# Hash attention with a gated feed-forward: where VectorE's decoding of the float64 weights stands in the order

## The chip, the cores and the metric

One core of one Trainium2 chip. The metric is the device time of one execution in microseconds; before the change it is 758.06, the median of three runs (755.7 to 759.31). TensorE (PE) multiplies and transposes, VectorE (DVE), ScalarE (ACT) and GpSimd (POOL) do the elementwise work, SyncE (SP) issues most DMAs. Line numbers L are those of the kernel before, unless the text says that they are of the changed one.

## The reference, cut to what matters

```python
B, H, S, D = 4, 8, 768, 64            # q, k, v: float32
q_bucket = sum((q @ proj > 0) * 2**arange(6));  k_bucket likewise
scores = where(q_bucket == k_bucket.T, q @ k.T / 8, -1e9)
attn = softmax(scores)                # + 1e-9 in the denominator
x = (attn @ v), heads side by side    # (4, 768, 512)
h = relu(x @ w_in)                    # d_ff = 1024
conv = 3-tap convolution of h along the sequence, one tap triple per channel
out = (h * sigmoid(conv)) @ w_out
```

w_in (512 x 1024), the taps and w_out (1024 x 512) arrive as float64. [...]

## The kernel before

**Attention.** The 32 heads are worked in 16 pairs, batch by batch (four pairs make a batch of the input). A pair is 12 *units*: six tiles of 128 queries for each of the two heads, in an order that takes two tiles of one head, two of the other. The main loop runs over units i; in step i it issues, in this order,
- the scores of unit i (`products`, L253: two passes of two matmuls; the second pass carries the low parts and the hash bits, so that a pair of different buckets gets a very low score),
- its row maximum on VectorE, which also moves the scores to SBUF (L266), and the scaled negative of it (L270),
- the transposes of unit i - 3 (L296) and their eviction `at` on ScalarE (L303),
- the exponential of unit i on ScalarE (L273),
- every fourth step, (i - 3) % 4 == 0, a *batch* of products with the values of the four units before (`values`, L322), 24 matmuls; for the first six pairs two transposes that spread the reciprocals of the sums go ahead of them (L317), and x = values times reciprocals follows (L331 on VectorE from the factors rs that ScalarE copied, L327; L332 and L333 on GpSimd make its high and low parts xh and xl). Later pairs are "late": they are normalised before the transposes (L281) and need no spread.

Scores, transposes and hash products share a ring of three PSUM buffers ("S"): the next user of a buffer waits until VectorE or ScalarE has read the last one.

**The next pair's operands.** R holds q and k of one pair, transposed; there is one buffer of it. `prepare` splits R into a high part hi and a low part that overwrites R (L171, L176, GpSimd; DMAs on SP put the parts into Q1, K1, Q2, K2), and multiplies R with the hash projections (`hash`, L186 on TensorE; L189 on VectorE turns the signs to bits, L191 on GpSimd scales them, eight DMAs place them). It goes forward one of seven steps per unit, from unit PREP of a pair on: unit 3 in the first, 2 in the second, 1 in the others. Six units after its start the pair's v and the pair after next's R are asked for; the load of R waits for the last DMA out of the buffer.

**Decoding.** Sixteen blocks of raw weights (128 x 512 float64, 512 KB each) and the taps. For a block, `decode` issues: its size, the absolute value of the high words, on ScalarE (L87); on VectorE five steps: L89 zeroes too small numbers, L91 shifts, L93 joins sign and exponent bits to the shifted mantissa (that is the upper part `up`), L95 keeps the power of two, L97 makes the lower part from the low words. `split_weight` then casts `up` to the high part on ScalarE (L105) and makes the low part in two GpSimd instructions (L107, L109). `background` is called once per unit after the values and lets the blocks under way go on until a step that waits for another engine; a new block begins every 4.1 units (RATE) from unit 6 (W0) on. So the five steps of VectorE stand one or two at a time behind the maxima of several units. The raw loads are issued on SP in units 2, 6, 10, ....

**The feed-forward** of a batch (`ffn`) follows two pairs after its last pair: 16 groups of 12 matmuls (`hidden`, L360), three behind them 9 matmuls each of `output` (L390), with the elementwise work of gate and split between. It runs four times. Blocks that aren't decoded by the first go on in it.

Of the kernel before, what the change touches and what calls it, by code (L numbers as in the profile page):

```python
# [7 lines left out]
F32 = mybir.dt.float32  # L8
# [20 lines left out]
F64_MIN = 2.0 ** -15 * 1.125  # L29
# [5 lines left out]
PREP = (3, 2, 1)  # L35
PREP_N = 6
W0 = 6
RATE = 4.1
HRATE = 2.5
# [4 lines left out]
def lsh_attention_conv_ffn(ctx, tc, qk, v, hw, w_in, conv_w, w_out, consts, ident_in, out):  # L44
# [29 lines left out]
    def decode(raw, n, name):  # L74

        pr = raw.rearrange("p (n two) -> p n two", two=2)
        lo, hi = pr[:, :, 0].bitcast(U32), pr[:, :, 1].bitcast(F32)
        up, low = (ring(wp, bufs, [P, WC], I32, f"w{x}", f"w{x}{name}")[:, :n]
                   for x, bufs in (("u", 3), ("l", 3)))
        upf, lowf = up.bitcast(F32), low.bitcast(F32)
        V = nc.vector
        nc.scalar.activation(lowf, hi, AF.Abs)  # L87
        yield 2
        V.scalar_tensor_tensor(upf, lowf, F64_MIN, hi, ALU.is_ge, ALU.mult)  # L89
        yield 1  # L90
        V.tensor_scalar(low, up, 3, 0x3FFFFFFF, ALU.logical_shift_left, ALU.bitwise_and)  # L91
        yield 0
        V.scalar_tensor_tensor(up, up, -0x40000000, low, ALU.bitwise_and, ALU.bitwise_or)  # L93
        yield 2
        V.tensor_scalar(low, up, -0x800000, None, ALU.bitwise_and)  # L95
        yield 0
        V.scalar_tensor_tensor(lowf, lo, 2.0 ** -52, lowf, ALU.mult, ALU.mult)  # L97
        return upf, lowf

    def split_weight(raw, name):  # L100

        up, low = yield from decode(raw, WC, name)
        yield 2
        blk = weights[name] = cp.tile([P, 2, WC], F32R, tag=f"w{name}", name=f"w{name}")
        nc.scalar.copy(blk[:, 0, :], up)  # L105
        yield 2
        nc.gpsimd.tensor_tensor(up, up, blk[:, 0, :].bitcast(F32), ALU.subtract)  # L107
        yield 1
        nc.gpsimd.tensor_tensor(blk[:, 1, :], up, low, ALU.add)  # L109

    def decode_taps(raw):
        up, low = yield from decode(raw, NFC * 3, "cw")
        nc.vector.tensor_tensor(cw.rearrange("p f k -> p (f k)"), up, low, ALU.add)
# [5 lines left out]
    fetched, splits, step = [], [], [0]  # L119

    def fetch(n):

        for src, name in blocks[:n]:
            raw = cp.tile([P, 2 * WC], I32, tag=f"w{name}", name=f"raw{name}")
            nc.sync.dma_start(raw, src)
            fetched.append((raw, name))
        del blocks[:n]

    def background(rate, stop):

        step[0] += 1
        if rate and fetched and step[0] // rate > (step[0] - 1) // rate:
            splits.append(split_weight(*fetched.pop(0)))
        now = splits[:]
        while now:
            for g in now[:]:
                ended = next(g, None)
                if ended is None:
                    splits.remove(g)
                if ended is None or ended >= stop:  # L140
                    now.remove(g)


    class Pair:
# [61 lines left out]
        def prepare_now(self):  # L206
# [10 lines left out]
            for h in range(2):  # L217
# [9 lines left out]
                bits = ring(wp, 3, [P, WC], I32, "wl", f"bits{nm}_{h}").bitcast(F32)[:, :HS]  # L227
# [78 lines left out]
    def values(pr, qb, ats, rec):  # L306
# [22 lines left out]
        def out():  # L329
            x = ring(wp, 2, [P, QB], F32, "x32", f"x{pr.nm}_{qb}")  # L330
# [14 lines left out]
        rs = ring(wp, 2, [P, QB], F32, "rs", f"rs{pr.nm}_{qb}")  # L345
# [35 lines left out]
    def output(b, half, f, g, acc):  # L381
# [10 lines left out]
        if f == NFC - 1:  # L392
            for m in range(HS // P):
                osb = ring(wp, 3, [P, WC], I32, "wu", f"osb{b}_{half}_{m}").bitcast(F32)
# [9 lines left out]
    def ffn(b, xs, fill, last):  # L404
# [4 lines left out]
        for i in range(len(todo) + FLAG):  # L409
# [8 lines left out]
            background(HRATE, 2)  # L418
# [27 lines left out]
    for i in range(n + LAG):  # L446
# [5 lines left out]
        for high, low in lows:  # L452
            high()
# [108 lines left out]
```

## Time and profile before

| what | value |
|---|---|
| runs | 755.7, 759.31, 758.06 us; median 758.06 |
| the profiled execution's own time | 758.92 us |
| its span, first to last instruction | 757.1 us |
| granted TensorE clock, mean | 0.99 |
| busy: PE, DVE, ACT, POOL | 717.0, 498.0, 511.9, 358.1 us |
| chain that ended last, by engine | PE 77%, DVE 15%, ACT 2%, DMA 2%, POOL 2% |
| first feed-forward begins | at 210.2 us |

A row of the timeline has the start, the length, the engine, the line, the operation, what it writes and reads, and in brackets the engine's idle time before it and what ended that. A row of the waits has who waited for whom, the total, how often, and the longest. In the table of busy times by stretch, each engine's busy us and count follow the stretch's length; the clock, the busy share of the DMA engines and GB/s end the row. The matmuls' ends are modelled.

### The profile page before, as it was taken

To read this page: it belongs to the slowest core of one execution; us is meant where nothing else is said; L and a number is where in the kernel's file an instruction comes from. 1 tells how busy PE (TensorE), PEld (TensorE's weight loads), DVE (VectorE), ACT (ScalarE), POOL (GpSimd) and SP (SyncE) were. 2 spreads that over 40 slices of the span, in tenths; PEclk is the share of its full clock that TensorE was granted. 3 is DMA by queue.
4 is the path that set the end of the run, shared out by engine and by line. 5 is a ranking of instruction groups with operands and counts; after the bars stand their busy time and mean duration, and the time that the engine had idled before them with its cause. 6 is when DMAs were issued, how large, how long until landed. Compare 5 with 4: busy or idle time off the path is not lost.

```text
span 757.1 us, 13345 instructions
## 1 busy us (share of the span) xinstructions
PE 717.0 (95%) x4588; PEld 586.6 (77%) x4588; DVE 498.0 (66%) x1212; ACT 511.9 (68%) x954; POOL 358.1 (47%) x355
## 2 busy tenths in 40 slices
PE   5989989888889999999999999999999999999997
PEld 3867767666679887777779988777779998778986
DVE  7778979778757646566657665666656665554653
ACT  5867777776755558778775547778775556875554
POOL 4345856565555324655735323556653433441222
PEclk8999999999999999999999999999999999999999
DMA  4656486482622103365541302256461211000011
GB/s 139 158 175 199 112 203 172 121 232 67 158 50 63 63 1 105 75 166 153 126 119 34 95 1 104 50 149 154 111 159 40 63 43 62 3 1 1 0 43 42
DMA packets 30355, 72.16 MB, mean 95 GB/s; under 512 B 5936, under 2 KB 7504, under 8 KB 30288
## 3 DMA queue, kind: packets, MB, share of 16 engines
q1 hardware_dynamic: 30000, 71.27, 34.8%
q8 instruction: 36, 0.59, 0.3%
q14 instruction: 31, 0.25, 0.1%
q10 hardware_dynamic: 288, 0.05, 0.0%
HBM read 27.40 MB, written 6.29 MB: 45 GB/s over the span
## 4 chain that ended last, share of the span: by engine, by line
PE 77%; DVE 15%; ACT 2%; DMA 2%; POOL 2%; issue 1%; DVEq 0%; SPq 0%; POOLq 0%; ACTq 0%
PE o L390 18%; PE h L360 17%; PE v L322 15%; PE s L253 13%; PE t L296 13%; DVE e L266 6%; DMA R<-in_qk 2%; PE hash L186 1%; DVE wuo L93 1%; DVE wlo L97 1%; DVE wui L93 1%; DVE st L270 1%; ACT e L273 1%; DVE wli L97 1%; DVE x L331 1%
## 5 line engine op out<-in xcount | busy, mean ns | idle before, releaser
L266 DVE TENSOR_SCALAR_CACHE_REDUCE e<-s 128x768 f32<-128x768 f32 x192 | 183.0, 953 | 87.3 <-PE s L253 80.8
L273 ACT ACTIVATE e<-e,st 128x768 f32<-128x768 f32 x192 | 180.7, 941 | 28.5 <-DVE st L270 13.9
L303 ACT COPY at<-t 128x768 f32<-128x768 f32 x192 | 152.0, 792 | 62.7 <-PE t L296 62.7
L296 PE MATMUL t<-ident,e 128*128 128x128 f32 x1152 | 162.6, 278 | 16.6 <-DVE e L266 14.0
L281 POOL TENSOR_SCALAR e<-e,st 128x768 f32<-128x768 f32 x120 | 109.2, 910 | 126.1 <-ACT at L303 65.0
L296 PEld LDWEIGHTS t<-ident,e 128*128 128x128 f32 x1152 | 130.9, 142 | 43.4 <-DVE e L266 23.7
L369 DVE SCALAR_TENSOR_TENSOR ht<-ht,cw 128x384 f32<-128x384 f32 (+1 forms) x128 | 113.1, 883 | 72.5 <-ACT ht L367 70.3
L379 POOL TENSOR_TENSOR g<-ht,g 128x384 fp32r<-128x384 f32 x64 | 72.9, 1138 | 169.3 <-ACT g L378 137.3
L390 PE MATMUL o<-wo,g 128*128 128x512 f32 x576 | 143.0, 394 | 1.0 <-POOL g L379 1.0
L360 PE MATMUL h<-xh,wi 128*128 128x386 f32 x512 | 142.2, 341 | 1.3 <-ACT ht L365 1.3
L322 PE MATMUL v<-at,v 128*64 128x256 f32 x1152 | 138.1, 385 | 0.0
L390 PEld LDWEIGHTS o<-wo,g 128*128 128x128 f32 x576 | 107.2, 188 | 22.0 <-POOL g L379 1.4
L253 PE MATMUL s<-K,Q 128*128 128x384 f32 x384 | 116.2, 384 | 3.9 <-DVE e L266 2.7
L322 PEld LDWEIGHTS v<-at,v 128*64 128x64 f32 x1152 | 83.2, 138 | 41.6 <-issue 9.2
L253 PE MATMUL s<-k,q 96*128 96x384 f32 x384 | 99.6, 340 | 2.5 <-DVE e L266 2.2
L360 PEld LDWEIGHTS h<-xh,wi 128*128 128x128 f32 x512 | 94.1, 188 | 5.3 <-ACT ht L365 1.8
L372 ACT ACTIVATE ht<-ht 128x384 f32<-128x384 f32 x64 | 33.6, 526 | 90.2 <-DVE ht L369 90.2
L360 PE MATMUL h<-xl,wi 128*128 128x386 f32 x256 | 86.8, 339 | 0.0
L253 PEld LDWEIGHTS s<-K,Q 128*128 128x128 f32 x384 | 58.5, 191 | 33.5 <-issue 18.6
L253 PEld LDWEIGHTS s<-k,q 96*128 96x128 f32 x384 | 70.6, 191 | 3.6 <-ACT q L233 3.1
L373 DVE TENSOR_TENSOR ht<-ht 128x384 f32<-128x384 f32 x64 | 43.1, 674 | 33.9 <-ACT ht L372 33.9
L176 POOL TENSOR_TENSOR R<-R,hi 128x768 fp32r<-128x768 f32 x30 | 59.2, 1973 | 0.2
(75 smaller groups left out, 613.5 us busy)
## 6 DMA issues: line engine op xcount, KB each, us to landing
R<-in_qk SPq DMA_DIRECT2D x15, 768.0 KB
K<-hi SPq DMA_DIRECT2D x60, 192.0 KB
v<-in_v SPq DMA_DIRECT2D x16, 384.0 KB
out<-osb SPq DMA_DIRECT2D x24, 256.0 KB
Q<-hi SPq DMA_DIRECT2D x30, 192.0 KB
q<-hi SPq DMA_DIRECT2D x30, 192.0 KB
Q<-R SPq DMA_DIRECT2D x30, 192.0 KB
k<-R SPq DMA_DIRECT2D x30, 192.0 KB
```

Of the source, the lines that this page charges most:

```text
L176: nc.gpsimd.tensor_tensor(lo, R, hi.bitcast(F32), ALU.subtract)
L253: nc.tensor.matmul(self.sp[:, half, :HS], A[:, h, qs], C[:, h, half * HS:(half + 1) * HS], start=(kk == 0), stop=(kk == 1))
L266: nc.vector.tensor_scalar(self.e.rearrange("p (a b) -> p a b", a=2), self.sp[:, :, :HS], MASKED, None, ALU.max, ALU.max, accum_out=self.st ...
L273: nc.scalar.activation(self.e, self.e, AF.Exp, bias=self.st[:, 1:2], scale=SCALE, accum_out=self.sum)
L281: nc.gpsimd.tensor_scalar(self.e, self.e, self.st[:, 3:4], 0.0, ALU.mult, ALU.add)
L296: nc.tensor.transpose(self.tp[:, c // 3, c % 3 * P:(c % 3 + 1) * P], self.e[:, c * P:(c + 1) * P], ident)
L303: nc.scalar.copy(pr.at[self.h][:, :, :, self.tq * P:(self.tq + 1) * P], self.tp[:, :, :3 * P].rearrange("p j (c q) -> p j c q", c=3))
L322: nc.tensor.matmul(av[h * D:(h + 1) * D, :QB], vt[:, c, h, :], ats[h][:, c // 3, c % 3, :], start=(c == 0), stop=(c == NCK - 1), tile_posi ...
L360: nc.tensor.matmul(hp[:, :HW], w, x[:, c0:c0 + HW], start=(n == 0), stop=(n == 3 * NCC - 1))
L369: nc.vector.scalar_tensor_tensor(t[:, a:z], ht[:, o + k - 1 + a:o + k - 1 + z], cw[:, f, k:k + 1], t[:, a:z], ALU.mult, ALU.add)
L379: nc.gpsimd.tensor_tensor(g[:, 1, :], t, g[:, 0, :].bitcast(F32), ALU.subtract)
L390: nc.tensor.matmul(op, l, r, start=(f == 0 and n == 0), stop=(f == NFC - 1 and n == 2))
```

## The change

- **Decoding in four steps and at one place.** L89 goes. The size is clamped on GpSimd instead (`clamp`), the shift works on the clamped size, and the join takes sign and exponent from the raw high words. The four steps of VectorE are issued only in the units of a batch, 3.75 in the mean (so four, every fourth time three), behind x and the hash bits and ahead of the next unit's maximum, from unit 7 on. Sizes run two blocks ahead, clamps one or two; a block's two GpSimd instructions (`ends`) are issued behind the next block's join.
- **x** (or the low part of a late pair) moves from the unit ahead of the batch into the batch's unit. Its ring and that of the factors have one buffer.
- **The hash** stands ahead of the values in the batch's unit: `prepare` starts at unit 1 in every pair, the hash is in its third step, together with the first low half; R and v are asked for at unit 7. Where a feed-forward comes at a pair's unit 2, the hash falls into it.
- **Raw loads** are issued by ScalarE, in units 1, 3, 5, 7 and then with each batch.
- The rings of `up` and of the sizes have 2 and 5 buffers instead of 3 and 3; the output staging moves from the one to the other.

```diff
-PREP = (3, 2, 1)
+PREP = 1
-W0 = 6
-RATE = 4.1
-HRATE = 2.5
+W0 = 7
+RATE = 3.75
...
-        V.scalar_tensor_tensor(upf, lowf, F64_MIN, hi, ALU.is_ge, ALU.mult)
...
+        def clamp(self):
+            nc.gpsimd.tensor_scalar(self.lowf, self.lowf, F32_MAX, F64_MIN, ALU.min, ALU.max)
+        def upper(self):
+            V, up, low = nc.vector, self.up, self.low
+            V.tensor_scalar(low, low, 3, 0x3FFFFFFF, ALU.logical_shift_left, ALU.bitwise_and)
+            yield
+            V.scalar_tensor_tensor(up, self.hi, -0x40000000, low, ALU.bitwise_and, ALU.bitwise_or)
+            yield
+        def lower(self):
+            V, up, low = nc.vector, self.up, self.low
+            V.tensor_scalar(low, up, -0x800000, None, ALU.bitwise_and)
+            yield
+            V.scalar_tensor_tensor(self.lowf, self.lo, 2.0 ** -52, self.lowf, ALU.mult, ALU.mult)
+            yield
+    def split_weights():
...
+        while todo:
+            d = todo.pop(0)
+            ahead()
+            yield from d.upper()
+            if ends:
+                ends()
+            if len(todo) == 2:
+                todo[-1].clamp()
+            yield from d.lower()
+            blk = weights[d.name] = cp.tile([P, 2, WC], F32R, tag=f"w{d.name}", name=f"w{d.name}")
+            nc.scalar.copy(blk[:, 0, :], d.upf)
+
+            def ends(d=d, blk=blk):
+                nc.gpsimd.tensor_tensor(d.upf, d.upf, blk[:, 0, :].bitcast(F32), ALU.subtract)
+                nc.gpsimd.tensor_tensor(blk[:, 1, :], d.upf, d.lowf, ALU.add)
...
-            nc.sync.dma_start(raw, src)
+            nc.scalar.dma_start(raw, src)
...
-            for now in ((sa, hs), (hs,), (sa,), (), (sb,), (), (sb,)):
+            for now in ((sa,), (), (hs, sa), (hs,), (sb,), (), (sb,)):
...
-            x = ring(wp, 2, [P, QB], F32, "x32", f"x{pr.nm}_{qb}")
+            x = ring(wp, 1, [P, QB], F32, "x32", f"x{pr.nm}_{qb}")
...
-            background(HRATE, 2)
+            background(1)
...
-        for high, low in done:
-            low()
+        if burst:
+            for high, low in lows:
+                low()
+            lows = []
+        if u and k == PREP and pi + 1 < len(pairs):
+            prep[0] = pairs[pi + 1].prepare()
+        next(prep[0], None)
...
+        if burst and i >= W0:
+            background(RATE)
...
-        if i >= W0 - 4:
-            fetch(i % 4 == 2)
-        if i >= 1:
-            background(RATE if i >= W0 else 0, 1)
+        fetch(i % 2 if i < 8 else burst)
```

VectorE's order before, around the first units of the third pair (names: e_2_1_1 is pair 2, query tile 1, head 1; bits_3 the hash bits of pair 3; wu, wl a block's upper and lower parts; the batch of the values is in the unit of e_2_1_1):

```order
L331 TENSOR_TENSOR x_1_1_866<-v_1_1_783,rs_1_1_784 128x256
L189 TENSOR_SCALAR bits_3_881<-hash_3_876,cst 128x384
L266 TENSOR_SCALAR e_2_0_1_894,st_2_0_1_893<-s_2_0_1_888 128x768
L270 TENSOR_SCALAR st_2_0_1_893<-st_2_0_1_893 128x1
L89 SCALAR_TENSOR_TENSOR wui_1_885<-wli_1_886,rawi_1_654 128x512
L266 TENSOR_SCALAR e_2_1_1_927,st_2_1_1_926<-s_2_1_1_921 128x768
L270 TENSOR_SCALAR st_2_1_1_926<-st_2_1_1_926 128x1
L91 TENSOR_SCALAR wli_1_886<-wui_1_885 128x512
L93 SCALAR_TENSOR_TENSOR wui_1_885<-wui_1_885,wli_1_886 128x512
L266 TENSOR_SCALAR e_2_2_0_969,st_2_2_0_967<-s_2_2_0_962 128x768
```

The same place on VectorE in the changed kernel, by its own lines (L299 is the maximum, L364 x, L222 the bits, L95, L97, L102 and L104 the four steps):

```order
L299 TENSOR_SCALAR e_2_1_1_910,st_2_1_1_909<-s_2_1_1_904 128x768
L303 TENSOR_SCALAR st_2_1_1_909<-st_2_1_1_909 128x1
L364 TENSOR_TENSOR x_1_1_924<-v_1_1_788,rs_1_1_789 128x256
L222 TENSOR_SCALAR bits_3_933<-hash_3_928,cst 128x384
L95 TENSOR_SCALAR wli_1_583<-wli_1_583 128x512
L97 SCALAR_TENSOR_TENSOR wui_1_582<-rawi_1_456,wli_1_583 128x512
L102 TENSOR_SCALAR wli_1_583<-wui_1_582 128x512
L104 SCALAR_TENSOR_TENSOR wli_1_583<-rawi_1_456,wli_1_583 128x512
L299 TENSOR_SCALAR e_2_2_0_974,st_2_2_0_972<-s_2_2_0_967 128x768
```

x, the bits and all four steps of a block stand between two maxima, where before one or two steps stood behind each. GpSimd's order in that same unit of the changed kernel (L365 and L366 are xh and xl, L209 the low half, L139 and L140 a block's ends, L90 a clamp, L224 the bits):

```order
L365 TENSOR_SCALAR xh_1_663<-x_1_1_924 128x256
L366 TENSOR_TENSOR xl_1_664<-x_1_1_924,xh_1_663 128x256
L209 TENSOR_TENSOR R_3_722<-R_3_722,hi_3_0_878 128x768
L139 TENSOR_TENSOR wui_0_452<-wui_0_452,wi_0_952 128x512
L140 TENSOR_TENSOR wi_0_952<-wui_0_452,wli_0_453 128x512
L90 TENSOR_SCALAR wli_1_955<-wli_1_955 128x512
L224 TENSOR_SCALAR bits_3_933<-bits_3_933,cst 128x384
```

Everything that GpSimd has to do for x, the next pair and a block follows on x in one run.

TensorE there before (hash_3 is pair 3's hash, t a unit's transposes, v_1_2 the batch):

```order
L186 MATMUL hash_3_876<-R_3_724,hw_sb 32x384 x4
L253 MATMUL s_2_0_1_888<-K_2_375,Q_2_374 128x384 x2
L253 MATMUL s_2_0_1_888<-k_0_75,q_0_73 128x384 x2
L296 MATMUL t_1_5_1_897<-ident,e_1_5_1_791 128x128 x6
L253 MATMUL s_2_1_1_921<-K_2_375,Q_2_374 128x384 x2
L253 MATMUL s_2_1_1_921<-k_0_75,q_0_73 128x384 x2
L296 MATMUL t_2_0_0_930<-ident,e_2_0_0_830 128x128 x6
L317 MATMUL v_1_2_919<-ident,rec_1_5_1_855 128x128 x2
```

And in the changed kernel:

```order
L286 MATMUL s_2_0_1_884<-K_2_340,Q_2_339 128x384 x2
L286 MATMUL s_2_0_1_884<-k_0_75,q_0_73 128x384 x2
L329 MATMUL t_1_5_1_893<-ident,e_1_5_1_796 128x128 x6
L286 MATMUL s_2_1_1_904<-K_2_340,Q_2_339 128x384 x2
L286 MATMUL s_2_1_1_904<-k_0_75,q_0_73 128x384 x2
L329 MATMUL t_2_0_0_913<-ident,e_2_0_0_844 128x128 x6
L219 MATMUL hash_3_928<-R_3_722,hw_sb 32x384 x4
L350 MATMUL v_1_2_902<-ident,rec_1_5_1_867 128x128 x2
```

The hash has moved behind two units' scores, directly ahead of the batch.

More of the change, by code (lines that the diff above doesn't have):

```diff
@@ L72, in lsh_attention_conv_ffn @@
     nc.vector.memset(zero[64:96], 0.0)
[L74 to L109, printed above, removed]
-    def decode_taps(raw):
-        up, low = yield from decode(raw, NFC * 3, "cw")
-        nc.vector.tensor_tensor(cw.rearrange("p f k -> p (f k)"), up, low, ALU.add)
+    class Decode:
+        def __init__(self, raw, n, name):
+            pr, self.name = raw.rearrange("p (n two) -> p n two", two=2), name
+            self.lo, self.hi = pr[:, :, 0].bitcast(U32), pr[:, :, 1]
+            self.up, self.low = (ring(wp, bufs, [P, WC], I32, f"w{x}", f"w{x}{name}")[:, :n]
+                                for x, bufs in (("u", 2), ("l", 5)))
+            self.upf, self.lowf = self.up.bitcast(F32), self.low.bitcast(F32)
+        def size(self):
+            nc.scalar.activation(self.lowf, self.hi.bitcast(F32), AF.Abs)
+        def clamp(self):
[12 more added lines that the diff above has]
+            yield
@@ new lines, in split_weights, with ahead @@
+    def split_weights():
+        todo, ends = [], None
+        def ahead():
+            if fetched:
+                raw, name = fetched.pop(0)
+                todo.append(Decode(raw, WC, name))
+                todo[-1].size()
+        ahead()
+        ahead()
+        yield
+        for d in todo:
+            d.clamp()
+        yield
+        while todo:
+            d = todo.pop(0)
+            ahead()
+            yield from d.upper()
[9 more added lines that the diff above has]
+                nc.gpsimd.tensor_tensor(blk[:, 1, :], d.upf, d.lowf, ALU.add)
+        ends()
@@ L116, in lsh_attention_conv_ffn @@
+    def decode_taps(raw):
+        d = Decode(raw, NFC * 3, "cw")
+        d.size()
+        yield
+        d.clamp()
+        yield
+        yield from d.upper()
+        yield from d.lower()
+        nc.vector.tensor_tensor(cw.rearrange("p f k -> p (f k)"), d.upf, d.lowf, ALU.add)
     blocks = [(w_in[c * P:(c + 1) * P, 2 * n * WC:2 * (n + 1) * WC], f"i{c}_{n}")
@@ L124, in fetch, with background @@
             raw = cp.tile([P, 2 * WC], I32, tag=f"w{name}", name=f"raw{name}")
-            nc.sync.dma_start(raw, src)
+            nc.scalar.dma_start(raw, src)
             fetched.append((raw, name))
         del blocks[:n]
[L129 to L141, printed above, removed]
+    def background(n):
+        due[0] += n
+        while due[0] >= 1:
+            due[0] -= 1
+            next(weights_todo, None)
     class Pair:
@@ L450, in lsh_attention_conv_ffn @@
         pi, k = divmod(i, 2 * NCK)
-        done, outs, lows = lows, [], outs
-        for high, low in lows:
+        burst = AVS[(i - LAG) % 4] > 0
+        for high, low in outs:
             high()
+        lows, outs = lows + outs, []
         wi = (i - LAG) // (2 * NCK)
@@ L458, in lsh_attention_conv_ffn @@
         if ending:
-            for high, low in done + lows:
+            for high, low in lows:
                 low()
-            done, lows = [], []
+            lows = []
         if u:
```

25 lines of the change are left out of this document (14 added, 11 removed).

## The prediction

> **What bounds the kernel now.** I read the page's engine line, then two stretches (the table of busy times by stretch), then the chain and the waits of the first 205 us.
>
> ```profile
> PE 717.0 (95%) x4588; PEld 586.6 (77%) x4588; DVE 498.0 (66%) x1212; ACT 511.9 (68%) x954; POOL 358.1 (47%) x355
> 140.00:160.00 20.00, 16.73 (x125) 13.10 (x124) 15.65 (x34) 14.33 (x27) 15.43 (x15) 1.00 0.54 131
> 300.00:320.00 20.00, 20.00 (x155) 14.92 (x154) 12.20 (x48) 15.90 (x31) 12.29 (x14) 1.00 0.25 58
> ```
>
> TensorE is busy 20.00 of 20 us in the late stretch, where all weights are decoded: nothing that VectorE gives up there can be gained. In the early stretch it is busy 16.73, with VectorE at 15.65 and GpSimd at 15.43. The change can pay only before the first feed-forward stage. There the waits are:
>
> ```profile
> PEld t L296 <- DVE e L266: 23.7, 29, 1.8
> PE t L296 <- DVE e L266: 14.0, 17, 1.4
> DVE wuo L89 <- ACT wlo L87: 9.3, 8, 1.4
> ```
>
> TensorE's next transposes need the PSUM buffer that a unit's maximum (L266) has read, and the maximum stands behind decoding. I measure this stage in periods: from one batch of products with the values to the next, four units later. Each batch begins with two spread transposes (L317).
>
> ```profile
> 24.29 0.38 PE L317 MATMUL v<-ident,rec 128*128 128x128 f32 x2
> 33.19 0.38 PE L317 MATMUL v<-ident,rec 128*128 128x128 f32 x2
> 47.45 0.63 PE L317 MATMUL v<-ident,rec 128*128 128x128 f32 x2
> 212.42 0.38 PE L317 MATMUL v<-ident,rec 128*128 128x128 f32 x2
> L317 PE MATMUL v<-ident,rec x36: 271/273/421, 24.3 to 212.5; 128*128 128x128 f32 x36
> ```
>
> 36 transposes are 18 batches, so 17 periods in 212.42 - 24.29 = 188.1 us, 11.07 each. The first, 33.19 - 24.29 = 8.90, has almost no decoding and no wait: that is TensorE's own price for four units and a batch. The second, 14.26, holds the worst stall:
>
> ```profile
> 39.93 0.38 SPq L158 DMA_DIRECT2D R<-in_qk  x1
> 44.21 0.85 PE L186 MATMUL hash<-R,hw_sb 128*32 128x384 f32 x8 [2.79 <-DMA R<-in_qk]
> ```
>
> If nothing but TensorE counted, the 17 periods would be 17 x 8.90, five hashes of 0.85 (the sixth goes into the feed-forward) and one hidden group in the last period:
>
> ```profile
> 388.75 2.11 PE h L360 x12
> ```
>
> 151.3 + 4.3 + 2.1 = 157.7. At most 30.4 us can be had.
>
> **What sets a period after the change.** VectorE's order in a batch's unit becomes: maximum, x, (hash bits), up to four decode steps, next maximum. TensorE covers this for a while: the batch, the next scores, one set of transposes and another scores. Then it needs the next maximum. So I work out when the decode steps end, first from their prices alone:
>
> ```profile
> 35.63 0.69 DVE L93 SCALAR_TENSOR_TENSOR wui<-wui,wli 128x512 int32<-128x512 int32 x1
> 38.46 0.42 DVE L95 TENSOR_SCALAR wli<-wui 128x512 int32<-128x512 int32 x1
> 38.92 0.69 DVE L97 SCALAR_TENSOR_TENSOR wli<-rawi,wli 128x512 f32<-128x512 uint32 x1
> ```
>
> A block now has two shifts or masks (0.42) and two three-operand steps (0.69): 2.22 us. The removed L89 had the shape of L97. But those rows ran with GpSimd idle. With GpSimd at work:
>
> ```profile
> 45.05 1.28 POOL L107 TENSOR_TENSOR wui<-wui,wi 128x512 f32<-128x512 f32 x1
> 45.21 0.62 DVE L189 TENSOR_SCALAR bits<-hash,cst 128x384 fp32r<-128x384 f32 x1 [2.88 <-DMA rawi<-in_w_in]
> 45.74 1.14 DVE L89 SCALAR_TENSOR_TENSOR wui<-wli,rawi 128x512 f32<-128x512 f32 x1
> 46.32 1.02 POOL L191 TENSOR_SCALAR bits<-bits,cst 128x384 fp32r<-128x384 f32 x1
> 46.80 0.94 DVE L266 TENSOR_SCALAR_CACHE_REDUCE e<-s 128x768 f32<-128x768 f32 x1
> 47.30 1.27 POOL L109 TENSOR_TENSOR wi<-wui,wli 128x512 fp32r<-128x512 f32 x1
> 47.86 0.99 DVE L91 TENSOR_SCALAR wli<-wui 128x512 int32<-128x512 int32 x1
> 48.53 2.01 POOL L176 TENSOR_TENSOR R<-R,hi 128x768 fp32r<-128x768 f32 x1
> 48.89 2.20 DVE L93 SCALAR_TENSOR_TENSOR wui<-wui,wli 128x512 int32<-128x512 int32 x1
> ```
>
> L93 takes 2.20 instead of 0.69: it ends 0.55 behind L176 (51.09 against 50.54). L91 ends 0.28 behind L109 (48.85 against 48.57). GpSimd's next instruction is stretched in turn: L191 ends 0.46 behind L89. The two engines take turns, instruction by instruction. The maximum and the bits, which read PSUM, run at their price all through. So a decode step that meets GpSimd costs the rest of GpSimd's instruction plus 0.28 or 0.55, and after it GpSimd's next instruction goes first.
>
> The Trainium skill (SBUF — State Buffer, section "Who interferes with whom") speaks against bunching the steps: VectorE and GpSimd share one port pair under an exclusive lock, the loser "fully blocks", and a VectorE instruction with at most one SBUF input outside the two-port modes stays free. By uncontended prices alone the sum would reach the 30.4 us above; by that rule whole GpSimd instructions come between the steps, and the sum is the smaller one below. The trace agrees (2.20 beside 0.69, and 0.94 for the maximum).
>
> The other prices, and how GpSimd is filled at that moment:
>
> ```profile
> 55.30 0.17 DVE L287 TENSOR_SCALAR sums<-sums 128x4 f32<-128x4 f32 x1
> 55.60 0.41 DVE L331 TENSOR_TENSOR x<-v,rs 128x256 f32<-128x256 f32 x1
> 56.24 0.41 POOL L332 TENSOR_SCALAR xh<-x 128x256 fp32r<-128x256 f32 x1
> 56.73 0.73 POOL L333 TENSOR_TENSOR xl<-x,xh 128x256 fp32r<-128x256 f32 x1
> L176 POOL TENSOR_TENSOR R<-R,hi x30: 1822/1844/2332, 22.9 to 595.6; 128x768 fp32r<-128x768 f32 x30
> ```
>
> From the start of the maximum: it and its scale 1.06 (46.80 to 47.86), x 0.41, so 1.47. GpSimd's queue behind x is xh (0.41), xl (0.73), then in two batches of three a low half (1.83), then the end of the block before (1.28 and 1.27) and a clamp.
> - *Hash batch* (low half, bits first): bits wait for TensorE's transposes and hash, so the steps begin at 2.25; xl ends at 2.7. Then 0.28 = 3.0, low half 4.8, 0.55 = 5.35, first end 6.65, 0.28 = 6.9, second end 8.2, 0.55 = 8.75.
> - *Batch with a low half, no hash*: one step free 1.9, xh 2.3, 0.55 = 2.85, xl 3.6, 0.28 = 3.85, low half 5.7, 0.55 = 6.25.
> - *Plain batch*: the same with the first end in place of the low half, 5.7.
>
> From there three maxima (3 x 1.06) and the sums (0.30 from 55.30 to 55.60) must still be done before the next batch's maximum: 3.48. Periods: 12.25, 9.75 and 9.2; TensorE's floor is 8.90 (9.75 with a hash).
>
> **The sum.** At 3.75 steps a batch every fourth batch has three: without a hash it falls to the floor, with one it ends at 6.9, period 10.4. Seventeen periods: the first two at the floor (one decode step; then no block's end yet) 17.8; four full hash batches 49.0; one with three steps 10.4; four with a low half 39.0; two at the floor 17.8; three plain 27.6; the last, three steps and the hidden group, 11.0. Total 172.6, against 188.1: **-15.5**.
>
> *Hash and loads.* Pair 2's R is loaded two units earlier and its hash comes one unit later, behind transposes and ahead of the values: the 2.79 and the slow restart behind it (the spread took 0.63, not 0.38) go; both are inside the 14.26. Late next is the low half on GpSimd, which waits for the hash; that is in the hash batch.
>
> *Raw weights on ScalarE's queue.* Four loads fall into the first eight units, two before, and no longer queue behind R:
>
> ```profile
> 1.18 0.45 ACTq L65 DMA_DIRECT2D cst<-in_consts  x1
> 12.71 0.39 SPq L158 DMA_DIRECT2D R<-in_qk  x1
> 13.15 0.47 SPq L125 DMA_DIRECT2D rawi<-in_w_in  x1
> 17.43 0.80 PE L186 MATMUL hash<-R,hw_sb 128*32 128x384 f32 x4 [0.41 <-DMA R<-in_qk]
> ```
>
> The hash waits for R at 17.43. The first raw load is now issued about 14.6 (behind an exponential); if it takes half the engines from then on, R lands up to 17.4 - 14.6 = 2.8 later; if it keeps behind R, 0. I take 1.0, near the lower end since most of R has moved by then: **+1.0**. The Trainium skill (DMA: Bandwidth & Descriptors, "Queues, rings and completion order") says that each DMA engine goes round-robin over the queue rows; by it the term would lie nearer 2.8 and the sum 1.8 smaller. No run here shows two such queues at once. Each issue also holds ScalarE about 0.45 us, 16 times; it falls into the batch, where ScalarE waits for the values anyway; bare, 7.2 us, but only a period already bound by ScalarE would feel it. SP loses 16 issues that delayed R and hi: nothing.
>
> *Sizes, casts, clamps, rings.* The size moves two blocks ahead, so the 9.3 us that L89 waited for ScalarE's L87 are not on the path. The cast still waits for VectorE's upper half; queued behind it on ScalarE are a size, the DMA issue, the factors rs and the next eviction.
>
> ```profile
> 41.70 0.60 ACT L105 CAST wi<-wui 128x512 fp32r<-128x512 f32 x1
> 42.21 0.66 ACT L87 ACTIVATE wli<-rawi 128x512 f32<-128x512 f32 x1
> ```
>
> In the hash batch the upper half is there at 5.35, so these end at 7.1 (0.60 + 0.66 + 0.45); the eviction's buffer is wanted by scores after 9: nothing. On GpSimd the low half's wait holds the block's ends, the clamp, the bits and the reciprocals for the next spread; clamp and bits (at most 1.02 each, from L191) and reciprocals (0.41, as xh) end by 11.2, before the next batch at 12.25: nothing, unless the period shrinks. The one-buffer x and rs rings are reused a whole batch later: nothing.
>
> *Feed-forward.* Pairs 7, 11 and 15 hash inside it: TensorE-bound on both sides, zero for the last two; the first adds 0.85 there and loses the late entry,
>
> ```profile
> 216.88 0.45 PE L360 MATMUL h<-xh,wi 128*128 128x386 f32 x1 [1.34 <-ACT ht L365]
> ```
>
> whose cause (VectorE behind with decoding) is gone: **-0.5**.
>
> Together -15.5 + 1.0 - 0.5 = -15.0. The profiled execution took 758.92, 0.86 above the median 758.06; so about **743 us**.
>
> **The rivals.**
> - *Full cover.* GpSimd's queue is mostly empty when the steps run (its work spreads out, 15.43 of 20 leaves room); the steps cost 2.22 and end by 4.5. For it: uncontended rows exist. Against: x itself starts GpSimd's run in the same unit. 758.1 - 30.4 + 0.5 = 728.
> - *Loads late.* The hash now stands ahead of the values and both wait for R, whose load follows a low half that GpSimd does late. A 2.8 us wait in each of five hash batches gives back 14: 757, no change. For it: 39.93 to 44.21. Against: hash two units later.
> - *Slower.* The turn-taking makes every batch like the hash batch: the steps end at 8.75 each time, VectorE is late by 3 us at the third scores. 15 periods at 12.25 plus the first (8.9) and last (11.0) are 203.7, or 15.5 more than before: 774. It decides once these 15 average over 11.4; before they average (188.1 - 8.9 - 11.95) / 15 = 11.15. The last period's 11.95 is its batch at 200.47 to 212.42:
>
> ```profile
> 200.47 0.38 PE L317 MATMUL v<-ident,rec 128*128 128x128 f32 x2
> ```
>
> **How the numbers follow.** Forecast 0.57, full cover 0.22, loads late 0.12, slower 0.09. A measurement here tells about 0.5% (3.8 us) from no change: faster 0.79, same 0.12, slower 0.09. The range runs from just below full cover, 727, to 756, short of the late loads; it leaves out the late loads (0.12) and the slower case (0.09), 0.2 in all.
>
> **What would show it.** Right: periods alternate, hash batches near 12, the others under 10; decode steps of 0.7 to 2.5 us between GpSimd's instructions; no wait of the hash for R at 44; late stages unchanged at 20.00 of 20. Wrong: all periods near 9 (cover), hash rows waiting for R (loads), or periods all over 11.4 (slower). A longer span behind 300 us would refute the premise itself.

## The result, and the profile after

The changed kernel takes 751.12 us (median of four runs, 748.77 to 752.14), the kernel before 758.68 beside it: a ratio of 0.9901, 95% interval 0.9878 to 0.9924. So it is faster by 7.6 us, about 1% and clear of the noise, but half of the 15 forecast. The profiled execution took 750.76 instead of 758.92, with a span of 749.0.

From here on L numbers are those of the changed kernel: L95, L97, L102, L104 are VectorE's four steps (they make the upper and lower float32 part of a block from the high and low 32-bit words of its float64 numbers), L299 the maximum, L329 the transposes, L350 the spread that begins a batch, L139 and L140 a block's ends, L90 the clamp, L209 the low half, L336 the eviction of the transposes on ScalarE. First the engines of the page after the change, then three stretches from the table by stretch:

```profile
PE 714.4 (95%) x4588; PEld 587.5 (78%) x4588; DVE 499.2 (67%) x1195; ACT 509.2 (68%) x954; POOL 373.6 (50%) x372
```

```profile
140.00:160.00 20.00, 19.55 (x154) 15.56 (x152) 18.02 (x41) 17.33 (x34) 14.80 (x14) 1.00 0.58 159
...
180.00:200.00 20.00, 16.46 (x107) 13.61 (x108) 12.09 (x28) 12.55 (x23) 12.51 (x13) 0.84 0.47 126
...
300.00:320.00 20.00, 20.00 (x154) 15.62 (x153) 13.29 (x54) 16.06 (x31) 13.91 (x15) 1.00 0.40 97
```

VectorE has 17 instructions fewer and is busy 1.2 us longer: L89's 21.2 us are gone, but the four steps that are left of each of the sixteen blocks take 65.4 us together where they took 50.4, and the feed-forward's convolution takes 4.7 more. TensorE is busy 19.55 of 20 from 140 to 160 (16.73 before): there the change does what it should. From 180 to 200 it is busy 16.46, at a clock of 0.84. In the late stretch TensorE is busy 20.00 of 20, as before. The periods, from the timeline of TensorE:

```profile
24.45 0.38 PE L350 MATMUL v<-ident,rec 128*128 128x128 f32 x2
36.92 0.38 PE L350 MATMUL v<-ident,rec 128*128 128x128 f32 x2
47.75 0.44 PE L350 MATMUL v<-ident,rec 128*128 128x128 f32 x2
...
157.28 0.38 PE L350 MATMUL v<-ident,rec 128*128 128x128 f32 x2
170.46 0.44 PE L350 MATMUL v<-ident,rec 128*128 128x128 f32 x2
183.42 0.38 PE L350 MATMUL v<-ident,rec 128*128 128x128 f32 x2
197.37 0.38 PE L350 MATMUL v<-ident,rec 128*128 128x128 f32 x2
207.13 0.38 PE L350 MATMUL v<-ident,rec 128*128 128x128 f32 x2
```

17 periods take 182.7 us: 5.4 less than before, not 15.5. The first two take 23.3 together (forecast 17.8), the eleven from 47.75 to 157.28 109.5 (forecast 112.6), the three from 157.28 to 197.37 40.1 (forecast, a plain one, one with a hash and one with a low half: 9.2 + 12.25 + 9.75 = 31.2), the last 9.8 (forecast 11.0). So the middle as a whole came out a little better than forecast, and both ends did not. The waits of this stage:

```profile
PEld t L329 <- DVE e L299: 22.4, 14, 3.9
PE t L329 <- DVE e L299: 17.9, 13, 3.5
...
DVE wuo L97 <- POOL wo L140: 8.0, 3, 4.3
...
DVE wli L95 <- POOL wli L90: 4.6, 1, 4.6
```

The last two are new, and each belongs to one of the two ends. The transposes' wait for the maximum, which the change was to take away, has not shrunk: 17.9 us in 13 waits, against 14.0 in 17 before. What shrank are waits at the hash. The list of before has these two, and of the change only 1.0 us is left of them:

```profile
PE hash L186 <- ACT wi L105: 3.0, 1, 3.0
PE hash L186 <- DMA R<-in_qk: 2.8, 1, 2.8
```

The scores' wait for the maximum, 2.7 before, is gone too. In the timeline of the change:

```profile
27.19 1.83 POOL L209 TENSOR_TENSOR R<-R,hi 128x768 fp32r<-128x768 f32 x1
...
29.11 1.19 POOL L90 TENSOR_SCALAR wli<-wli 128x512 f32<-128x512 f32 x2
...
29.75 0.82 DVE L95 TENSOR_SCALAR wli<-wli 128x512 int32<-128x512 int32 x1 [4.62 <-POOL wli L90]
...
40.74 0.39 SPq L191 DMA_DIRECT2D R<-in_qk  x1
...
190.73 0.69 DVE L97 SCALAR_TENSOR_TENSOR wuo<-rawo,wlo 128x512 int32<-128x512 int32 x1 [4.29 <-POOL wo L140]
...
192.35 0.33 PE L329 MATMUL t<-ident,e 128*128 128x128 f32 x1 [3.54 <-DVE e L299]
```

In the first batch VectorE waits 4.62 us for a clamp, which stands behind a low half on GpSimd; the maximum behind the shift comes late, and TensorE waits 1.75 us at 31.59. At 190.73 the join L97 waits 4.29 us for the end L140 of the block two before, because both use one of the two buffers of `up`; the maximum behind it comes late, and TensorE waits 3.54 us.

Why only then: at 3.75 steps a batch, the order slips by one step, a quarter of a block, every fourth batch. Once a batch runs L102, L104 of block n + 1 and then L95, L97 of block n + 2, the ends of block n have only just been queued, in the same batch, behind xh, xl and, in two of the three, a low half.

### The profile page after: what moved, and what is told of

The parts are those of the page before. It is cut to its first block, busy times and chain, and to the rows that moved or that the text cites. A ratio compares the mean times of both kernels' runs of the same rounds, so it can differ in the third digit from the quotient of the medians.

```text
span 749.0 us, 13385 instructions
## 1 busy us (share of the span) xinstructions
PE 714.4 (95%) x4588; PEld 587.5 (78%) x4588; DVE 499.2 (67%) x1195; ACT 509.2 (68%) x954; POOL 373.6 (50%) x372
## 4 chain that ended last, share of the span: by engine, by line
PE 69%; DVE 4%; POOL 4%; DMA 3%; ACT 1%; issue 1%; SPq 0%; POOLq 0%; DVEq 0%
PE o L423 18%; PE h L393 17%; PE s L286 11%; PE t L329 11%; PE v L355 11%; DVE e L299 2%; DMA k<-R 1%; DMA R<-in_qk 1%; PE hash L219 1%; POOL wuo L139 1%; POOL e L314 1%; POOL wo L140 1%; ACT e L306 1%; DVE wuo L97 1%; POOL R L209 1%
## 5 line engine op out<-in xcount | busy, mean ns | idle before, releaser
L299 DVE TENSOR_SCALAR_CACHE_REDUCE e<-s 128x768 f32<-128x768 f32 x192 | 183.3, 955 | 80.9 <-PE s L286 72.1
L336 ACT COPY at<-t 128x768 f32<-128x768 f32 x192 | 152.3, 794 | 47.3 <-PE t L329 47.1
L329 PE MATMUL t<-ident,e 128*128 128x128 f32 x1152 | 164.5, 280 | 19.9 <-DVE e L299 17.9
L314 POOL TENSOR_SCALAR e<-e,st 128x768 f32<-128x768 f32 x120 | 109.3, 911 | 117.3 <-ACT at L336 59.9
L329 PEld LDWEIGHTS t<-ident,e 128*128 128x128 f32 x1152 | 133.4, 144 | 42.6 <-DVE e L299 22.4
L402 DVE SCALAR_TENSOR_TENSOR ht<-ht,cw 128x384 f32<-128x384 f32 (+1 forms) x128 | 117.8, 921 | 70.0 <-ACT ht L400 66.8
L355 PE MATMUL v<-at,v 128*64 128x256 f32 x1152 | 134.9, 383 | 0.0
L286 PE MATMUL s<-K,Q 128*128 128x384 f32 x384 | 118.7, 391 | 1.0 <-POOL K L253 0.9
L355 PEld LDWEIGHTS v<-at,v 128*64 128x64 f32 x1152 | 78.7, 137 | 45.5 <-issue 10.9
L286 PE MATMUL s<-k,q 96*128 96x384 f32 x384 | 102.2, 348 | 2.2 <-DVE e L299 2.2
L286 PEld LDWEIGHTS s<-K,Q 128*128 128x128 f32 x384 | 60.1, 196 | 22.2 <-issue 17.4
L286 PEld LDWEIGHTS s<-k,q 96*128 96x128 f32 x384 | 72.9, 197 | 3.0 <-ACT q L266 3.0
L406 DVE TENSOR_TENSOR ht<-ht 128x384 f32<-128x384 f32 x64 | 41.5, 649 | 31.5 <-ACT ht L405 31.3
L209 POOL TENSOR_TENSOR R<-R,hi 128x768 fp32r<-128x768 f32 x30 | 60.4, 2014 | 0.9 <-PE hash L219 0.8
```

Source lines behind the costliest of these rows:

```text
L209: nc.gpsimd.tensor_tensor(lo, R, hi.bitcast(F32), ALU.subtract)
L286: nc.tensor.matmul(self.sp[:, half, :HS], A[:, h, qs], C[:, h, half * HS:(half + 1) * HS], start=(kk == 0), stop=(kk == 1))
L299: nc.vector.tensor_scalar(self.e.rearrange("p (a b) -> p a b", a=2), self.sp[:, :, :HS], MASKED, None, ALU.max, ALU.max, accum_out=self.st ...
L314: nc.gpsimd.tensor_scalar(self.e, self.e, self.st[:, 3:4], 0.0, ALU.mult, ALU.add)
L329: nc.tensor.transpose(self.tp[:, c // 3, c % 3 * P:(c % 3 + 1) * P], self.e[:, c * P:(c + 1) * P], ident)
L336: nc.scalar.copy(pr.at[self.h][:, :, :, self.tq * P:(self.tq + 1) * P], self.tp[:, :, :3 * P].rearrange("p j (c q) -> p j c q", c=3))
```

## The experiments

All ratios are to the kernel before; e1 to e4 ran beside runs of it at 757.65, e5 to e8 at 757.17, e9 to e11 at 758.07.

| run | median us | ratio, 95% interval |
|---|---|---|
| the change | 751.12 | 0.9901 (0.9878 to 0.9924) |
| e1_up3 | 747.22 | 0.9866 (0.9845 to 0.9886) |
| e2_first2 | 748.63 | 0.9883 (0.9862 to 0.9903) |
| e3_whole | 743.69 | 0.9813 (0.9785 to 0.9840) |
| e4_raw_sp | 759.85 | 1.0021 (0.9999 to 1.0044) |
| e5_ends_later | 730.84 | 0.9657 (0.9621 to 0.9693) |
| e6_before_clamp | 766.14 | 1.0108 (1.0078 to 1.0139) |
| e7_spread_steps | 741.09 | 0.9785 (0.9756 to 0.9814) |
| e8_thin_loads | 743.09 | 0.9807 (0.9779 to 0.9836) |
| e9_lows_off | 746.94 | 0.9863 (0.9835 to 0.9891) |
| e10_ends_and_lows | 748.66 | 0.9891 (0.9864 to 0.9918) |
| e11_ends_lows_thin | 751.60 | 0.9923 (0.9896 to 0.9949) |

**e1_up3: the upper parts' ring.**

```diff
-                                for x, bufs in (("u", 2), ("l", 5)))
+                                for x, bufs in (("u", 3), ("l", 4)))
...
```

> Theory R (ring): the late periods are long (13.18, 12.96 and 13.95 us, from the batch at 157.28 to that at 197.37) because the upper parts have two buffers: when the four steps of a batch have drifted to mask, product, shift, join, the join of a block waits in the same batch for GpSimd's end of the block two before it (2.53, 1.18 and 4.29 us). With three buffers of up (and four of the sizes, to keep the space) the waits go: these three periods fall to about 9.8 to 11 and the kernel to about 743 us. Rival T (turns): the periods are long because VectorE and GpSimd take turns there over more work; the three periods stay above 12 and the kernel at 751.

747.22, 3.9 below the change (the intervals just overlap), and not the 743 expected. The wait of L97 for L140 is gone, and the three late periods take 34.3 together instead of 40.1 (11.8, 13.3 and 9.3), but the buffer had to come from the sizes' ring, and a wait of ScalarE takes part of its place:

```profile
ACT wlo L87 <- POOL wo L140: 7.1, 2, 4.2
```

The same end L140 now holds a size instead of a join, and the fourth period grows from 9.7 to 13.8.

**e2_first2: the first batch without its shift**, which goes into the second batch as its fifth step.

```diff
-            background(RATE)
+            background(2 if i == 7 else 5.5 if i == 11 else RATE)
```

> Theory F (first shift): the first period, 12.47 us instead of 8.9, is long because the first batch also issues a block's first shift, which waits 4.62 us on VectorE for the clamp, the size and the raw load behind it. With two steps in that batch and five in the next, all else in its place, the first period falls to about 9 and the kernel by about 3 us, to 748. Rival D (DMA crowding): R of pair 2 is issued at 40.7 us whatever VectorE does, so the gain of the first period is given back in the next two, and the kernel stays at 751.

748.63, 2.5 below the change; the intervals overlap, so the periods say more than the kernel's time. The first takes 10.5 instead of 12.5, the first two 21.8 instead of 23.3. From the third batch on the order is the change's: L97 still waits 8.0 for L140, and the three late periods take 38.9.

**e3_whole: whole blocks.** The same for the first batch, and 4 steps in every other, so that no batch crosses from one block to the next.

```diff
-            background(RATE)
+            background(2 if i == 7 else 4)
```

> Two steps in the first batch, then four in every batch, so that each batch holds one whole block, shift, join, mask, product, and never the drifted order in which the join waits. If theories R and F both hold: the late three periods at 9.5 to 11, the first at 9, the kernel at about 741. If only F: 748. If only R: 744. If turn-taking alone sets the batches (T): a batch of four steps everywhere costs more than the three-step ones it replaces, 753.

743.69, 7.4 below the change, with two buffers of `up`. L97 no longer waits for L140: by the time of the next batch's join the ends are done. The periods from the 13th to the 16th are 9.7, 10.4, 10.3 and 9.8. The first two, with 22.7, are hardly better than the change's 23.3, and the eleven of the middle, now with four steps in every batch, take 115.8 instead of 109.5.

**e4_raw_sp: the raw loads back on SyncE.**

```diff
-            nc.scalar.dma_start(raw, src)
+            nc.sync.dma_start(raw, src)
```

> Only the raw loads go back to SyncE's queue. If the second DMA queue crowds R and hi early (theory D; DMA engines 0.86 busy from 20 to 40 us), pair 2's hash no longer waits 1.02 us for R and the kernel gains 1 to 2 us, 749.5. If instead SyncE's order is what held hi and R back, the raw loads stand in front of them again, R comes later and the kernel loses 1 to 4 us, 753. If ScalarE's issue time matters (16 x 0.33 us), a gain of at most 5 us spread over all periods.

759.85, 8.7 above the change; the profiled execution took 756.38, 5.6 above. One stall stands out, in the timeline and the waits:

```profile
42.14 1.01 PE L286 MATMUL s<-K,Q 128*128 128x384 f32 x2 [10.79 <-ACT at L336]
```

```profile
ACT wli L87 <- DMA rawi<-in_w_in: 11.5, 2, 9.6
```

The size on ScalarE waits 9.6 us for a raw block that stands behind the pair's loads on SyncE, the eviction queued behind it on ScalarE comes late, and the first period takes 22.3 (12.5 in the change). The sixteen periods behind it win back 4.9 of these 9.8, so the whole stage is 4.9 longer.

**e5_ends_later: GpSimd's ends and the clamp two units after the batch**, on e3_whole.

```diff
             if ends:
-                ends()
+                late_ends.append(ends)
             if len(todo) == 2:
-                todo[-1].clamp()
+                late_ends.append(todo[-1].clamp)
...
+        if (i - LAG) % 4 == 2:
+            for f in late_ends:
+                f()
+            late_ends.clear()
```

> Four whole steps a batch as in e3_whole (743.7 us), and GpSimd's two ends (L139, L140) and the clamp (L90) of a block are issued two units after the batch, where VectorE decodes nothing. Taking turns (theory): in the batch GpSimd then has only xh, xl and the low half, so the four steps end by about 5.5 instead of 8.75 us after the maximum; the batches with a hash, 10.6 to 12.7 us long in e3_whole, fall to 10 to 10.5, the others stay at 9.7 to 9.8; kernel 736 to 740. Rival A, no turn-taking that matters (the hash batch is long because the hash waits for R and the bits for the hash): hash batches keep 12 or more, kernel 742 to 745. Rival B, the ends that come later hold the next reciprocals or x up on GpSimd: spreads of the next batch wait, every batch grows, kernel over 746.

730.84: 12.9 below e3_whole, 26 below before, and below the range that was expected. The two timelines at the same batch, VectorE and GpSimd only. With the ends in the batch (e3_whole):

```profile
47.48 0.62 DVE L222 TENSOR_SCALAR bits<-hash,cst 128x384 fp32r<-128x384 f32 x1 [1.97 <-PE hash L219]
...
48.45 2.01 POOL L209 TENSOR_TENSOR R<-R,hi 128x768 fp32r<-128x768 f32 x1
...
48.82 2.19 DVE L97 SCALAR_TENSOR_TENSOR wui<-rawi,wli 128x512 int32<-128x512 int32 x1
50.42 1.73 POOL L139 TENSOR_TENSOR wui<-wui,wi 128x512 f32<-128x512 f32 x1
...
51.04 1.39 DVE L102 TENSOR_SCALAR wli<-wui 128x512 int32<-128x512 int32 x1
...
52.22 1.34 POOL L140 TENSOR_TENSOR wi<-wui,wli 128x512 fp32r<-128x512 f32 x1
...
52.47 1.65 DVE L104 SCALAR_TENSOR_TENSOR wli<-rawi,wli 128x512 f32<-128x512 uint32 x1
...
54.03 0.94 DVE L299 TENSOR_SCALAR_CACHE_REDUCE e<-s 128x768 f32<-128x768 f32 x1
...
55.04 0.33 PE L329 MATMUL t<-ident,e 128*128 128x128 f32 x1 [2.27 <-DVE e L299]
```

And with the ends later (e5_ends_later):

```profile
47.05 0.62 DVE L222 TENSOR_SCALAR bits<-hash,cst 128x384 fp32r<-128x384 f32 x1 [1.91 <-PE hash L219]
...
48.04 0.77 DVE L97 SCALAR_TENSOR_TENSOR wui<-rawi,wli 128x512 int32<-128x512 int32 x1
...
48.84 0.85 DVE L102 TENSOR_SCALAR wli<-wui 128x512 int32<-128x512 int32 x1
...
49.37 1.99 POOL L209 TENSOR_TENSOR R<-R,hi 128x768 fp32r<-128x768 f32 x1
...
49.72 2.18 DVE L104 SCALAR_TENSOR_TENSOR wli<-rawi,wli 128x512 f32<-128x512 uint32 x1
...
52.70 0.96 DVE L299 TENSOR_SCALAR_CACHE_REDUCE e<-s 128x768 f32<-128x768 f32 x1 [0.80 <-PE s L286]
```

In the first, each of the three steps ends 0.28 or 0.55 us behind a GpSimd instruction (51.01 and 50.46, 52.43 and 52.15, 54.12 and 53.56), as in the trace of before. From the bits' start to the last step's end it takes 54.12 - 47.48 = 6.6 us (the forecast had 8.75 - 1.63 = 7.1); the maximum comes late, TensorE waits. In the second the ends are not between the steps, and only the low half costs a step much: 51.90 - 47.05 = 4.9, and the maximum now waits for TensorE. All of VectorE is busy 483.1 us instead of 502.0, with the same instructions. The join still waits for the ends, 1.2 us at most each time, but no wait of TensorE for the maximum is over 0.5. The 17 periods take 168.4 instead of 178.4; what comes behind the last spread is as long as in e3_whole (540.2 and 540.1). What is left is mostly the hash: it waits for R 1.85 us at 46.1 and 1.78 at 105.8.

**e6_before_clamp: L89 alone.** The order of before; the size is clamped on GpSimd, and VectorE has four steps.

```diff
-        V.scalar_tensor_tensor(upf, lowf, F64_MIN, hi, ALU.is_ge, ALU.mult)
+        nc.gpsimd.tensor_scalar(lowf, lowf, F32_MAX, F64_MIN, ALU.min, ALU.max)
...
```

> The order of before (757.65 us), with L89 alone taken off VectorE: the size is clamped on GpSimd in its place. 16 steps of 0.69 us, 1.1 and more with GpSimd at work, leave VectorE. Theory (the stall is VectorE's steps behind the maxima, wherever they stand): about half of 16 x 1.1 counts, 748 to 752. Rival (the stall is the place of the steps and the order, not their number; the clamp also costs GpSimd 16 x 0.6 to 1.0 and VectorE waits for it where it waited for the size): 756 to 760, no change.

766.14, slower than before by 1.1%; both expectations fail. VectorE's first step waits for the clamp, and the next maximum stands behind it:

```profile
DVE wli L92 <- POOL wli L90: 11.7, 7, 2.1
```

So one step fewer is worth nothing by itself, with its clamp directly ahead of it. That size and clamp must run far ahead is argued from this wait; no run tries it in the order of before.

**e7_spread_steps: one step behind the maximum of every unit**, all else as changed.

```diff
-        if burst and i >= W0:
-            background(RATE)
+        if i >= W0:
+            background(2 if i == 7 else 1)
```

> The changed kernel (751.1 us) with one decode step behind the maximum of every unit in place of all steps in the batch's unit; x, hash, loads, clamps and sizes as changed. Theory (bunching is what pays: between batches the maxima run undisturbed): spread steps meet GpSimd's work in each unit, periods of 10 to 11 throughout, kernel 752 to 758. Rival (bunching is neutral or costs; what pays is one step fewer, the clamp off VectorE, sizes ahead and whole blocks): every period 9.5 to 10, hash batches too, kernel 738 to 743.

741.09, 10.0 below the change and 2.6 below e3_whole (their intervals overlap). The rival holds in the main: the steps' place is not what pays. The groups of the join, in the change and spread:

```profile
L97 DVE SCALAR_TENSOR_TENSOR wui<-rawi,wli 128x512 int32<-128x512 int32 x8 | 8.3, 1033 | 0.4
```

```profile
L97 DVE SCALAR_TENSOR_TENSOR wui<-rawi,wli 128x512 int32<-128x512 int32 x8 | 5.3, 668 | 0.0
```

Spread out, the join runs at its bare 0.67; in the batch it costs 1.03. The last step, L104, gains nothing to speak of (mean of all 1.18 instead of 1.21). TensorE nowhere waits 1 us or more in this stage, and the granted clock is 1.00 throughout. But its periods are even, 9.4 to 10.7, not below 10 as the rival had it; and queued together with GpSimd out of the way (e5), the steps do better still.

**e8_thin_loads: two raw loads fewer before 40 us**, on e3_whole.

```diff
-        fetch(i % 2 if i < 8 else burst)
+        fetch(i in (1, 4) or burst)
```

> As e3_whole (743.7 us), but the raw weights are asked for in units 1 and 4 and then with each batch, instead of units 1, 3, 5, 7 and then with each batch: two loads fewer before 40 us. Theory (early loads crowd the DMA engines: 0.86 of them busy from 20 to 40 us; R of pair 2 and the upper half's copies come late): the hash's wait for R at 46.5, 1.92, goes to under 0.5 and the first four periods lose 1 to 3 in all, kernel 741 to 743. Rival A (R is late because of SyncE's order and the one buffer of the high part, not the bytes): the wait stays, 743 to 745. Rival B (the third block now lands late, ScalarE's size waits for it and holds the evictions): a wait of ScalarE's L87 of over 2 us, kernel over 745.

743.09, the same as e3_whole. The split of R (L204), which waits for R, begins at 44.93 instead of 46.48, and the hash waits no more (the second period is 9.6 instead of 12.1). But R's load was itself issued at 40.72 instead of 41.97: of the 1.55 us only 0.3 are a faster load. And the first period grows from 10.6 to 12.5, with a wait of TensorE of 2.07 at 32.39: the stall has moved one batch ahead. So the theory of the bytes is not shown.

**e9_lows_off, e10_ends_and_lows, e11_ends_lows_thin: the low halves out of the batch too**, on e3_whole, on e5, and on e5 with the loads of e8.

```diff
-            for now in ((sa,), (), (hs, sa), (hs,), (sb,), (), (sb,)):
+            for now in ((sa,), (), (hs,), (hs, sa), (sb,), (sb,), ()):
```

> As e3_whole (743.7 us), with the two low halves of a pair (L209, 1.83 us each on GpSimd) issued one unit after a batch and two units before one, instead of in the two batches' units; the ends stay in the batch. Taking turns (theory): the hash batches lose the low half's 1.83 + 0.55 ahead of the steps' end, 12.1 to 12.7 go to about 10.3, batches of 10.3 go to 9.7; also R comes free one unit earlier, and the hash's wait for R (1.92 at 46.5) goes to under 1; kernel 735 to 739. Rival A (only the ends matter, because they also hold the upper parts' buffers): 742 to 745. Rival B (a low half between batches takes its turn with the maxima's neighbours and delays the reciprocals): 745 or more.

> e5_ends_later (730.8 us) with the low halves moved as in e9_lows_off. Taking turns (theory): in the batch GpSimd has only xh and xl, so all batches go to 9.3 to 9.8 and those with a hash to 9.8 to 10.2; the waits of the hash for R (1.85 at 46.1, 1.78 at 105.8 in e5_ends_later) shrink by the time by which R comes free earlier, 1 to 1.8 each; kernel 724 to 728. Rival (TensorE's floor is reached, the rest is R's load, which hangs on SyncE's order and not on the low half): 729 to 732.

> e10_ends_and_lows with the raw weights asked for in units 1 and 4 and then with each batch, two loads fewer before 40 us. If the loads' bytes still hold R up early, the first three periods lose another 1 to 2 and the kernel is 1 to 2 below e10; if the third block lands late (in e8_thin_loads the first period grew from 10.59 to 12.45), the first period grows by up to 2 and the kernel is 0 to 2 above e10.

746.94, 748.66 and 751.60: all three expectations fail in the kernel's time. (The edit puts a pair's second low half one unit ahead of a batch, not two as the expectation has it.) In the stage, e9 does what taking turns says (17 periods in 170.4 instead of 178.4; hash batches 9.2 to 10.3), though the second period is 13.9. The first takes 9.0 (10.6 in e3_whole); why was not taken apart. What follows is 11 us longer, 551.0 instead of 540.1. TensorE's waits behind 205 us, of e3_whole and of e9_lows_off:

```profile
PE t L329 <- POOL e L314: 1.8, 4, 0.9
```

```profile
PE t L329 <- POOL e L314: 11.4, 10, 1.6
```

The late pairs are normalised on GpSimd (L314) ahead of their transposes, and the low half now stands ahead of that. In e10 the same 11 us are lost late, and in the stage the ends, the clamp and the low half are queued in neighbouring units, so that GpSimd runs on into the next batch: 172.9 us instead of e5's 168.4. e11 is another 2.9 slower, beyond the 0 to 2 expected.

## Which parts of the prediction held, and which steps failed

**The stage: right in the main.** Of the span's 8.1 us, 5.4 are in the 17 periods and 2.8 behind the last spread, where the prediction had 0.5; the start lost 0.2. The gain of the stage is not the one that was forecast, though: TensorE waits 4.7 us less at the hash, of which the prediction names the 2.79; for the maximum it waits 3.9 more at the transposes and 2.7 less at the scores.

**Taking turns: right as the price of a step, and not as the price of a batch.** e3 and e5 show the first directly. The Trainium skill (SBUF — State Buffer, "Who interferes with whom"), by which VectorE and GpSimd shut each other out of a shared port pair, was used against the change; the trace agrees, 2.19 beside a bare 0.69, and e5 shows what the rule is worth when the order heeds it: 12.9 us. But that the middle periods came near their sum, 109.5 against 112.6, is partly luck: their four hash batches take 12.7, 10.4, 9.6 and 9.4, 5.1 less than forecast, and the other seven 2.0 more. The sign "hash batches near 12" holds for two of five (12.7 and 13.0), and in both of these the clock was halved for a while (last section). That the prediction took GpSimd's place in the batch as given, and not as the thing to move, is why its "full cover" had too small a basis. e5, at 730.84, is near the 728 of that rival, but not by full cover: its 17 periods take 168.4 where cover needs 157.7, and the stages behind the last spread are 4.5 shorter than before.

**The step that failed first: "the first two at the floor (one decode step; then no block's end yet) 17.8".** They took 23.3, +5.5; before the change they had taken 23.2. The first batch issues a shift that needs a clamp behind a low half, and was priced by its count alone; without that shift (e2) the first period falls from 12.5 to 10.5. The second period holds pair 2's hash, 0.85, and its wait for R, 1.02, which the sum left out there. How the rest comes about stays open: no run takes less than 20.2 for these two periods.

**The step that failed second: the batches of 3.75 steps were priced by their number ("every fourth batch has three"), without asking which steps stand together.** The ring of two `up` buffers stood in the diff and in no term. +8.9 in three periods: VectorE's join waits 2.53, 1.18 and 4.29 us there, and TensorE behind it 1.89, 2.49 and 3.54. Both runs that take the join's wait away shorten these periods, e1 to 34.3 and e3 to 30.5, where 31.2 was forecast. With the middle (-3.1) and the last period (-1.2) these two steps make up the 10.1 that the stage missed. That e3 lands on the forecast's 743 is luck: its stage takes 178.4, not 172.6, and 4.6 us went behind the last spread instead of 0.5.

**A price that no term had: the clock behind a stall.** The prediction saw a slow restart behind the 2.79 of before, and did not ask which new stall would bring another. The change has five of them in this stage and before it has two; at about 1.55 us each (an estimate, from the last section) that is some 4.7 us, inside the two steps above and the third period.

**"Pair 2's R is loaded two units earlier": wrong.** It was issued at 40.74 (39.93 before): two units earlier in the order, but not in time, since the load waits for the last DMA out of the one buffer. The hash still waits 1.02 us at 46.96.

**Raw on ScalarE's queue, +1.0: not where it was put.** The delay of pair 1's R that it stood for isn't there: the hash that waits for it starts at 17.28, 17.43 before. It may have come at pair 2: R takes 6.2 us there from its issue to its first reader (46.90), with a raw load issued on ScalarE's queue 0.15 ahead of it, and took 4.3 before, with the raw load behind it on the same queue. No run takes this one load away alone. The other way, e4 shows that with sizes two blocks ahead the queue is worth 8.7 us. "SP loses 16 issues: nothing" missed that. An issue held ScalarE 0.33 us, not 0.45.

**Feed-forward, -0.5: right in sign.** From the last spread to the end of the span it is 541.9 instead of 544.7. The wait of 1.34 us at its entry is gone, as forecast. 0.9 us are won by the end of the first feed-forward and 2.0 in the attention that follows it; why was not followed up.

**Not settled:** what the change's parts that go together (L89 off, sizes and clamps ahead) give without the batch was only seen from e6 and e7, not in the order of before. A second buffer of R, which would show whether e5's hash waits can go, was not tried.

## What to carry to other kernels

When steps of one engine are gathered at one place, list what the other engine on the same ports has queued there, and move that away first: here the placing alone gave nothing, and placing with GpSimd's ends moved gave 13 us. For each batch write down which steps of which block stand together, and for each ring the instruction that frees the buffer: a rate that isn't a whole block brings every alignment in turn, the worst one too. Where work runs ahead on an engine (here the sizes), see that what it waits for does not queue behind other loads, or it stops everything queued behind it, as in e4. And when you count a stall of TensorE, count the slower clock that can follow.

## What the runs showed of the hardware

A stall of TensorE can be paid twice. In the change, behind the wait of 2.49 at 178.41, the scores and the next transposes run slower:

```profile
178.41 0.88 PE L329 MATMUL t<-ident,e 128*128 128x128 f32 x6 [2.49 <-DVE e L299]
179.04 0.64 PE L286 MATMUL s<-K,Q 128*128 128x384 f32 x2
179.47 0.84 PE L286 MATMUL s<-k,q 96*128 96x384 f32 x2
180.11 1.48 PE L329 MATMUL t<-ident,e 128*128 128x128 f32 x6
181.25 0.99 PE L286 MATMUL s<-K,Q 128*128 128x384 f32 x2
182.03 0.84 PE L286 MATMUL s<-k,q 96*128 96x384 f32 x2
182.67 0.91 PE L329 MATMUL t<-ident,e 128*128 128x128 f32 x6
183.42 0.38 PE L350 MATMUL v<-ident,rec 128*128 128x128 f32 x2
```

From 178.41 to the spread it takes 5.01 us. In e3_whole the same seven pieces take 3.46 (117.82 to 121.28) behind a wait of 1.42, and 5.02 (55.04 to 60.06) behind one of 2.27: 1.55 more. The granted clock shows why: read in stretches of 1 us it is 0.72 from 179, 0.50 from 180 to 182, 0.57 from 182 and 1.00 again from 183, which is 3.4 us at half clock. In stretches of 20 us, one such piece lowers the mean to about 0.91:

```profile
20.00:40.00 20.00, 18.20 (x128) 14.65 (x126) 12.58 (x38) 15.43 (x28) 8.09 (x12) 0.91 0.86 210
40.00:60.00 20.00, 16.68 (x112) 13.56 (x111) 16.14 (x34) 14.09 (x26) 10.91 (x12) 0.91 0.56 164
160.00:180.00 20.00, 15.62 (x102) 12.33 (x99) 14.01 (x30) 11.75 (x22) 12.94 (x13) 0.90 0.46 129
```

Between the first and the last spread the change has five of them, behind waits of 1.75, 2.29, 1.89, 2.49 and 3.54 us; all three long periods hold one. Before the change there are two, behind waits of 2.79 and 1.44. The experiments have none (e7), one (e5, e9), two (e2, e3, e8), three (e1, e10), five (e6, e11) and six (e4, four of them in a row). The length of a wait does not decide alone: in e3_whole the wait of 2.27 at 55.04 is followed by one and that of 2.39 at 87.42 is not. No term of the prediction's sum had this for a new stall. The Trainium skill (TensorE: Matmul & The Clock Gate, "What's actually happening") says that the clock halves after an idle window of about 3.4 us, whose start the kernel doesn't set; the trace agrees on the half, and shows it behind waits that are shorter.
